# Memory-augmented attention and a spatial-gating MLP on one core: load phase reordered, half of a running sum moved ahead of the products with V

## The chip, the cores and the metric

The kernel runs on one core of a Trainium2 chip. The metric is the device time of one execution in microseconds (us), lower is better. Engines are named as in the profile: PE is TensorE (matmuls), PEld its weight loads, DVE is VectorE, ACT is ScalarE, POOL is GpSimd, SP is SyncE, which issues the DMAs. L514 is line 514 of the kernel.

## The reference

Block A is a recurrence over 64 segments of 32 tokens; 8 memory rows go ahead of each segment's tokens, and the first 8 rows of a segment's output are the memory of the next. Block B is an MLP with a gate that mixes over all 2048 tokens. Weights and activations are bfloat16; x is 2048 x 512, there are 32 heads of 128.

```python
for s in range(n_seg):
    xs = x[:, s * seg_len:(s + 1) * seg_len, :].copy()
    h = jnp.concatenate([mem, xs], axis=1)
    q = jnp.einsum('btd,dhe->bhte', h, Wq)
    k = jnp.einsum('btd,dhe->bhte', h, Wk)
    v = jnp.einsum('btd,dhe->bhte', h, Wv)
    scores = jnp.einsum('bhqe,bhke->bhqk', q, k) * scale
    scores = jnp.where(mask[None, None], scores, -1000000000.0)
    p = _softmax(scores, axis=-1)
    o = jnp.einsum('bhqk,bhke->bhqe', p, v)
    o = jnp.einsum('bhte,hed->btd', o, Wo)
    mem = o[:, :M, :].copy()
    outs.append(o[:, M:, :])
...
h = x + _A_ref(_layernorm(x, axis=-1), A_mem0, A_Wq, A_Wk, A_Wv, A_Wo, A_seg_len)
h2 = h + _B_ref(_layernorm(h, axis=-1), B_w_in, B_w_sp, B_b_sp, B_w_out)
```

## The kernel before

Every operation is written in one hand-made order. An `Emitter` records each operation with what it reads and writes, puts it at the end of its engine's list, and derives the semaphore waits. So an engine does its operations strictly in the order of the code, and the code's order is the schedule.

**Load phase.** `load_w` and `load_wh` bring Wq in quarters and Wk as two quarters and a half. Meanwhile PE computes, for the extension rows (the last 8 tokens of each segment, gathered for 16 segments in a "ck"), the Q and K products in 28 groups of 16 matmuls 128x128 (`qkx_mm`, L432): index n of the loop over `first` counts them. Groups 0 to 15 are Q, 16 to 27 are K. Each group writes one of four PSUM banks in turn, and its bank is emptied (`qkx_evac`) by ACT for even n (L441), by DVE for odd n (L443). So group n can begin only once group n-4 has been copied out. Between the groups DVE also normalizes three loaded blocks of x: `ln_stats` is a bn_stats (L379) and a bn_aggr (L380) on DVE followed by an add and a power on POOL (L381, L383); `ln_apply` (L389) on DVE needs POOL's result. A normalized block is turned by PE (`xT`, 16 matmuls, L397) and copied to the ring of x by ACT (`ring_copy`, `xe_copy`).

**Loop.** 64 iterations s, four to a row block rb = s // 4, with j4 = s % 4. In each, PE does the projections Q and K (L514 and L515 are one helper, `tile_mm`), the scores, two softmaxes (b = 0, 1), the projection V, and then this part, to which the change belongs:

- `ev`: one group of 16 matmuls from a list of work that is independent of the recurrence. It is `vx_group` for s = 1 to 7 and s = 10, 11, `qkx_group` for s = 8, 9, `qkr_group` for s = 12 to 43, and `z_group` (block B) from s = 44 until these run out, after s = 61.
- `PV_half(s, 0)` and `PV_half(s, 1)`: the products with V, for each half 16 matmuls 32x40 (L659) and 4 of 32x64 (L665). They need V (`V_evac`, L651 on DVE, L649 on ACT) and the normalized exponentials (L625, L631).
- `cT_evac`: four copies of 128x320 out of PSUM, 0 and 1 by ACT (L678), 2 and 3 by DVE (L680).
- `WoX_mm(rb - 1, j4)`, from s = 4 on: the first "ext output sum". The previous row block's extension rows are multiplied with Wo and summed in bank `WXB` over j4 = 0 to 3: eight matmuls of 512 columns (L743), four for each b. It reads `cTx`, which the four iterations of the row block before have filled.
- `late`: a group of four matmuls (`pour`). Where the `ev` group is a `vx_group`, it is done ahead of `ev`; else it stands here, behind `WoX_mm`.
- `Wo`: the output projection from `cT`, in the order 0, 2, 1, 3, in groups of four matmuls of 256 columns. The first group needs copy 0.

A matmul whose output has 32 rows stands in one of four column strips of the array; four of them, one per strip, run side by side and are called a group here.

**Places of the instruction stream.** `plan` (L1072) counts PE's instructions in blocks of `FETCH` = 256, and chooses for each iteration how many weight reloads (`spare`, four instructions each, 0 to 8 of them) to put in, so that a block's limit falls on certain places of the iteration. The instructions of an iteration that it assumes are written in it as a number.

## Time and profile before

| | |
|---|---|
| time, median of 3 runs | 840.41 us (838.03 to 840.58) |
| the profiled execution | 840.04 us, of which the span is 838.3 us |
| TensorE clock granted, mean | 0.999 |
| load phase, until the first matmul of the loop | 35.5 us |
| loop | 35.5 to about 683 us, about 9.9 us for an iteration |
| block B | from there to the end |

A row of the timeline has the start in us from the span's start, how long the merged row was busy, engine, line, operation, output and inputs, shape, count, and in brackets the idle time before it and what ended it. [...]

### The profile page before, as it was taken

To read this page: it belongs to the slowest core of one execution; us is meant where nothing else is said; L and a number is where in the kernel's file an instruction comes from. 1 tells how busy PE (TensorE), PEld (TensorE's weight loads), DVE (VectorE), ACT (ScalarE), POOL (GpSimd) and SP (SyncE) were. 2 spreads that over 40 slices of the span, in tenths; PEclk is the share of its full clock that TensorE was granted. 3 is DMA by queue.
4 is the path that set the end of the run, shared out by engine and by line. 5 is a ranking of instruction groups with operands and counts; after the bars stand their busy time and mean duration, and the time that the engine had idled before them with its cause. 6 is when DMAs were issued, how large, how long until landed. Compare 5 with 4: busy or idle time off the path is not lost.

```text
span 838.3 us, 45576 instructions
## 1 busy us (share of the span) xinstructions
PE 827.7 (99%) x22059; PEld 446.4 (53%) x19541; DVE 518.2 (62%) x1321; ACT 465.7 (56%) x1250; POOL 128.0 (15%) x340
## 2 busy tenths in 40 slices
PE   9999999999999999999999999999999999999997
PEld 9755555555555555555555555555555554444443
DVE  3556667666666666666666676666666667654443
ACT  3456665667666766667666666666666676500000
POOL 5011111111111111111111121111111113200000
PEclk9999999999999999999999999999999999999999
DMA  9962222323222212131223233233323389033001
GB/s 316 395 211 54 73 67 60 76 57 61 60 46 60 54 48 65 43 67 51 63 62 88 54 78 75 78 84 81 93 78 75 84 241 345 1 114 113 26 14 40
DMA packets 112407, 78.65 MB, mean 94 GB/s; under 512 B 65992, under 2 KB 103888, under 8 KB 112208
## 3 DMA queue, kind: packets, MB, share of 16 engines
q1 hardware_dynamic: 112208, 75.67, 31.7%
q8 instruction: 165, 2.70, 1.4%
q14 instruction: 34, 0.28, 0.1%
HBM read 43.16 MB, written 22.12 MB: 78 GB/s over the span
## 4 chain that ended last, share of the span: by engine, by line
PE 95%; DMA 1%; DVE 1%; ACT 1%; SPq 0%; issue 0%; POOL 0%
PE f_ps L514 47%; PE f_ps L1356 11%; PE f_ps L515 11%; PE f_ps L743 4%; PE f_ps L659 3%; PE f_ps L1480 3%; PE f_ps L1349 2%; PE f_ps L811 2%; PE f_ps L451 2%; PE f_ps L432 2%; DMA f_part<-in_A_x_dram 1%; PE f_ps L585 1%; PE f_ps L606 1%; PE f_ps L716 1%; PE f_ps L457 1%; PE f_ps L665 1%
## 5 line engine op out<-in xcount | busy, mean ns | idle before, releaser
L514 PE MATMUL f_ps<-f_arena,f_hT 128*32 128x512 bf16 (+1 forms) x5404 | 359.3, 351 | 0.3
L514 PEld LDWEIGHTS f_ps<-f_arena,f_hT 128*32 128x32 bf16 x5404 | 135.4, 96 | 138.7 <-issue 50.2
L551 ACT ACTIVATE f_Tst<-f_ps 128x512 bf16<-128x512 f32 x224 | 127.1, 597 | 65.3 <-PE f_ps L514 65.3
L515 PE MATMUL f_ps<-f_arena,f_hT 128*32 128x512 bf16 (+1 forms) x1764 | 146.7, 341 | 0.0
L514 PE MATMUL f_ps<-f_arena,f_cT 128*32 128x256 bf16 x3844 | 128.5, 272 | 0.9 <-ACT f_cT L678 0.5
L514 PEld LDWEIGHTS f_ps<-f_arena,f_cT 128*32 128x32 bf16 x3844 | 94.0, 96 | 28.9 <-ACT f_cT L678 19.6
L563 DVE STREAM_TRANSPOSE f_QT<-f_Tst 128x256 uint32<-128x256 uint32 x128 | 57.1, 446 | 72.2 <-ACT f_Tst L551 72.2
L1356 PE MATMUL f_ps<-f_arena 128*128 128x512 bf16 x448 | 101.0, 379 | 0.6 <-DVE f_arena L1342 0.4
L651 DVE CAST f_V_sb<-f_ps 128x512 bf16<-128x512 f32 (+1 forms) x128 | 71.0, 555 | 42.0 <-PE f_ps L514 42.0
L680 DVE TENSOR_SCALAR f_cT<-f_ps 128x320 bf16<-128x320 f32 x128 | 56.9, 487 | 28.6 <-PE f_ps L665 28.6
L1356 PEld LDWEIGHTS f_ps<-f_arena 128*128 128x128 bf16 x448 | 43.5, 98 | 54.0 <-DVE f_arena L1342 2.0
L599 ACT ACTIVATE f_E_sb<-f_ps 128x224 bf16<-128x224 f32 x128 | 46.2, 361 | 36.4 <-PE f_ps L591 36.4
L709 DVE CAST f_part<-f_ps 128x256 bf16<-128x256 f32 x64 | 27.2, 425 | 62.9 <-PE f_ps L514 62.9
L570 POOL COPY f_QT<-f_arena 128x128 uint32<-128x128 uint32 x64 | 18.8, 294 | 297.0 <-PE f_ps L591 296.9
L678 ACT ACTIVATE f_cT<-f_ps 128x320 bf16<-128x320 f32 x128 | 49.0, 435 | 23.0 <-PE f_ps L665 23.0
L721 ACT ACTIVATE f_hT<-f_ps 128x16 bf16<-128x16 f32 x126 | 23.2, 184 | 53.9 <-PE f_ps L716 53.4
L1362 DVE TENSOR_TENSOR f_arena<-f_ps,f_arena 128x512 f32<-128x512 f32 x28 | 19.3, 690 | 51.4 <-PE f_ps L1356 48.7
L575 DVE CAST f_ps<-f_mask 128x224 f32<-128x224 bf16 x128 | 47.1, 368 | 0.0
L621 ACT ACTIVATE f_R_sb<-f_R_sb 128x160 f32<-128x160 f32 x128 | 43.2, 338 | 4.1
L700 POOL COPY f_cTx<-f_cT 128x256 bf16<-128x256 bf16 x64 | 25.4, 398 | 121.7 <-DVE f_cT L680 121.7
L707 ACT ACTIVATE f_part<-f_ps 128x256 bf16<-128x256 f32 x64 | 24.6, 385 | 32.1 <-PE f_ps L514 32.1
L541 ACT ACTIVATE f_Tst<-f_ps 128x256 bf16<-128x256 f32 x128 | 42.1, 381 | 0.1
(130 smaller groups left out, 1206.9 us busy)
## 6 DMA issues: line engine op xcount, KB each, us to landing
wT_d<-f_wst SPq DMA_DIRECT2D x64, 128.0 KB, 2.7
f_arena<-wT_d SPq DMA_DIRECT2D x32, 256.0 KB, 4.9
f_arena<-in_A_Wv_dram SPq DMA_DIRECT2D x2, 2048.0 KB, 20.5
f_arena<-in_A_Wo_dram SPq DMA_DIRECT2D x8, 512.0 KB, 9.4
f_Vx<-vext_d SPq DMA_DIRECT2D x63, 64.0 KB, 2.4
f_arena<-in_A_Wq_dram SPq DMA_DIRECT2D x3, 1024.0 KB, 10.5
vext_d<-f_Vs SPq DMA_DIRECT2D x24, 128.0 KB, 2.2
z2p_d<-f_Vs SPq DMA_DIRECT2D x26, 112.0 KB, 1.9
```

The costliest lines, as they stand in the source:

```text
L514: return e.matmul(out, lhsT=lhsT, rhs=rhs, start=start, stop=stop, skip_group_check=True, tile_position=(0, 32 * c))
L515: return e.add_instruction(mybir.InstMatmult(name=nc.get_next_instruction_name(), ins=[e.lower_ap(rhs), e.lower_ap(lhsT)], outs=[e.lower_a ...
L541: act(lambda e: e.activation(out=Tst[:, 1, 256 * k:256 * k + 256].rearrange("p (gi r) -> p gi r", r=2), in_=ps[:, bank, 0:256].rearrange(" ...
L551: act(lambda e: e.activation(out=Tst[:, tb, :].rearrange("p (C gi r) -> p C gi r", C=2, r=2), in_=ps[:, bank, :].rearrange("p (C r gi) -> ...
L563: dve(lambda e: e.transpose(out=dst, in_=Tst[:, mi, :].bitcast(U32)), reads=[("T", mi, 0), ("T", mi, 1)], writes=wr)
L575: dve(lambda e: e.tensor_copy(out=ps[:, bank, 0:224], in_=mask[:, :]), reads=["mask"], writes=[PB(bank)])
L599: act(lambda e: e.activation(out=E_sb[:, b, :], in_=ps[:, bank, 0:224], func=ACT.Exp, scale=scale, bias=SHIFT), reads=[PB(bank)], writes=[ ...
L621: act(lambda e: e.activation(out=R_sb[:, b, :], in_=R_sb[:, b, :], func=ACT.Exp, scale=-1.0, bias=RBIAS), reads=[("R", b)], writes=[("R", b)])
L651: dve(lambda e: e.tensor_copy(out=V_sb[:, b, cs], in_=ps[:, bank, cs]), reads=[PB(bank)], writes=wr)
L678: act(lambda e: e.activation(out=dst, in_=src, func=ACT.Copy, scale=UNSC), reads=[PB(PVB[c])], writes=[("cT", c)])
L680: dve(lambda e: e.tensor_scalar(out=dst, in0=src, scalar1=UNSC, scalar2=None, op0=ALU.mult), reads=[PB(PVB[c])], writes=[("cT", c)])
L1356: pe(lambda e: e.matmul(ps[:, bank, 0:TB], lhsT=z2[:, sc, fb * 128:(fb + 1) * 128], rhs=wTb[tb % 2][:, :, sc, :], start=(n == 0), stop=(n ...
```

## The change

Load phase: the K groups of the two ck, which came as four of ck 0 and then four of ck 1, now alternate two by two. The three `ln_stats` move from behind groups 10, 11, 12 to behind 11, 12, 13, and the three `ln_apply` from behind 11, 12, 13 to behind 13, 14, 15, where they stand ahead of the `ln_stats` of the same n. The three turnings of x move from behind groups 15, 18, 21 to 17, 19, 22.

Loop: for s from 4 on, the left 256 columns of the first four of the eight matmuls of `WoX_mm` are done by four matmuls of their own (`WoX_first`) between `ev` and `PV_half(s, 0)`; the right 256 columns of the same four, and the other four at full width, stay behind the copies (`WoX_rest`). So there are 12 matmuls in the place of 8. The planner's count of an iteration rises from 592 to 600.

```diff
-    def WoX_mm(rb, qr):
-        for bg in range(8):
+    def WoX_first(rb, qr):
+        for g in range(4):
+            h = 4 * qr + g
+            pe(lambda e, h=h, g=g: e.matmul(ps[32 * g:32 * g + 32, WXB, 0:256], lhsT=cTx[:, rb % 2, 8 * qr + g, :], rhs=w_o[:, h, 0:256],
+                                            start=(qr == 0), stop=False, skip_group_check=True, tile_position=(0, 32 * g)),
+               reads=[("cTx", rb % 2), ("Wo", 0, qr)], writes=[PB(WXB)])
+
+    def WoX_rest(rb, qr):
+        for g in range(4):
+            h = 4 * qr + g
+            pe(lambda e, h=h, g=g: e.matmul(ps[32 * g:32 * g + 32, WXB, 256:512], lhsT=cTx[:, rb % 2, 8 * qr + g, :], rhs=w_o[:, h, 256:512],
+                                            start=False, stop=False, skip_group_check=True, tile_position=(0, 32 * g)),
+               reads=[("cTx", rb % 2), ("Wo", 0, qr)], writes=[PB(WXB)])
+        WoX_mm(rb, qr, range(4, 8))
+
+    def WoX_mm(rb, qr, bgs=range(8)):
+        for bg in bgs:
...
     first = [(ck, i) for i0 in range(0, 8, 2) for ck in range(2) for i in (i0, i0 + 1)]
-    first += [(0, i) for i in range(8, 12)] + [(1, i) for i in range(8, 12)] + [(0, i) for i in range(12, 16)]
+    first += [(ck, i) for i0 in (8, 10) for ck in range(2) for i in (i0, i0 + 1)] + [(0, i) for i in range(12, 16)]
...
+        if 13 <= n < 16:
+            ln_apply(n - 9)
         if 11 <= n < 14:
-            ln_apply(n - 7)
-        if 10 <= n < 13:
-            ln_stats(n - 6)
-        if n == 15:
+            ln_stats(n - 7)
+        if n == 17:
             xT(4, 6)
             ring_copy(0, 6)
-        if n == 18:
+        if n == 19:
             xT(5, 7)
             ring_copy(1, 7)
-        if n == 21:
+        if n == 22:
             xT(6, 6)
...
-        n = 592 + 24 * (s % 4 == 2) + 8 * (s >= 3 * CK)
+        n = 600 + 24 * (s % 4 == 2) + 8 * (s >= 3 * CK)
...
+        if rb > 0:
+            WoX_first(rb - 1, j4)
         PV_half(s, 0)
         PV_half(s, 1)
...
         if rb > 0:
-            WoX_mm(rb - 1, j4)
+            WoX_rest(rb - 1, j4)
```

DVE in the load phase, from its first copies of groups on. L443 are the copies of the odd groups. Before:

```order
L443 CAST f_arena<-f_ps 128x4x16x8 x5
L379 BN_STATS f_st<-f_part 128x6
L380 BN_AGGR f_mv<-f_st 128x2
L443 CAST f_arena<-f_ps 128x4x16x8
L389 TENSOR_SCALAR f_part<-f_part,f_mv,f_rs 128x512
L379 BN_STATS f_st<-f_part 128x6
L380 BN_AGGR f_mv<-f_st 128x2
L389 TENSOR_SCALAR f_part<-f_part,f_mv,f_rs 128x512
L379 BN_STATS f_st<-f_part 128x6
L380 BN_AGGR f_mv<-f_st 128x2
L443 CAST f_arena<-f_ps 128x4x16x8
L389 TENSOR_SCALAR f_part<-f_part,f_mv,f_rs 128x512
```

And now:

```order
L443 CAST f_arena<-f_ps 128x4x16x8 x6
L379 BN_STATS f_st<-f_part 128x6
L380 BN_AGGR f_mv<-f_st 128x2
L379 BN_STATS f_st<-f_part 128x6
L380 BN_AGGR f_mv<-f_st 128x2
L443 CAST f_arena<-f_ps 128x4x16x8
L389 TENSOR_SCALAR f_part<-f_part,f_mv,f_rs 128x512
L379 BN_STATS f_st<-f_part 128x6
L380 BN_AGGR f_mv<-f_st 128x2
L389 TENSOR_SCALAR f_part<-f_part,f_mv,f_rs 128x512
L443 CAST f_arena<-f_ps 128x4x16x8
L389 TENSOR_SCALAR f_part<-f_part,f_mv,f_rs 128x512
```

Between the copies of groups 11 and 13 stood two L389, each of which waits for POOL, and two pairs of statistics; now two pairs of statistics stand there and no L389.

PE in one iteration of the `qkr_group` kind, from the `ev` group (the L514 that reads f_hTe) to the first matmuls of `Wo` (the L514 that reads f_cT). Before:

```order
L514 MATMUL f_ps<-f_arena,f_hTe 32x512 x16
L659 MATMUL f_ps<-f_E_sb,f_V_sb 128x40 x16
L665 MATMUL f_ps<-f_E_sb,f_Vx 128x4x16 x4
L659 MATMUL f_ps<-f_E_sb,f_V_sb 128x40 x16
L665 MATMUL f_ps<-f_E_sb,f_Vx 128x4x16 x4
L743 MATMUL f_ps<-f_arena,f_cTx 32x512 x8
L451 MATMUL f_ps<-f_arena,f_hTe 32x512 x4
L514 MATMUL f_ps<-f_arena,f_cT 32x256 x32
```

And now (L742 is `WoX_first`, L749 the right half in `WoX_rest`, L758 `WoX_mm`):

```order
L514 MATMUL f_ps<-f_arena,f_hTe 32x512 x16
L742 MATMUL f_ps<-f_arena,f_cTx 32x256 x4
L659 MATMUL f_ps<-f_E_sb,f_V_sb 128x40 x16
L665 MATMUL f_ps<-f_E_sb,f_Vx 128x4x16 x4
L659 MATMUL f_ps<-f_E_sb,f_V_sb 128x40 x16
L665 MATMUL f_ps<-f_E_sb,f_Vx 128x4x16 x4
L749 MATMUL f_ps<-f_arena,f_cTx 32x256 x4
L758 MATMUL f_ps<-f_arena,f_cTx 32x512 x4
L451 MATMUL f_ps<-f_arena,f_hTe 32x512 x4
L514 MATMUL f_ps<-f_arena,f_cT 32x256 x32
```

Four matmuls of 256 columns now stand ahead of the products with V, and one group's half less stands between these and `Wo`.

More of the change, by code (lines that the diff above doesn't have):

```diff
@@ L743, in WoX_mm @@
             pe(lambda e, h=h, g=g, i=8 * qr + bg: e.matmul(ps[32 * g:32 * g + 32, WXB, :], lhsT=cTx[:, rb % 2, i, :], rhs=w_o[:, h, :],
-                                                           start=(i < 4), stop=(i >= H - 4), tile_position=(0, 32 * g)),
+                                                           start=(i < 4), stop=(i >= H - 4), skip_group_check=True, tile_position=(0, 32 * g)),
                reads=[("cTx", rb % 2), ("Wo", b, qr)], writes=[PB(WXB)])
```

## The prediction

> **What bounds the kernel now.** First the page: its span, the engines' shares, the chain that ended last.

> ```profile
> span 838.3 us, 45576 instructions
> PE 827.7 (99%) x22059; PEld 446.4 (53%) x19541; DVE 518.2 (62%) x1321; ACT 465.7 (56%) x1250; POOL 128.0 (15%) x340
> PE 95%; DMA 1%; DVE 1%; ACT 1%; SPq 0%; issue 0%; POOL 0%
> ```

> PE sets the end nearly everywhere, so an edit pays only where it removes time in which PE does not start the next matmul. The profiled execution took 840.04 us, 1.74 us of it outside the span; the median of three is 840.41, and single runs spread over 2.5 us. The sum below is made against 840.04.

> Second, PE's timeline of the load phase, between the eighth microsecond and the start of the loop.

> ```profile
> 8.37 13.62 PE L432 MATMUL f_ps<-f_hTe,f_arena 128*128 128x128 bf16 x240
> 21.92 0.41 PE L397 MATMUL f_ps<-f_ident,f_part 128*32 128x128 bf16 x16
> 22.26 1.07 PE L432 MATMUL f_ps<-f_hTe,f_arena 128*128 128x128 bf16 x16
> 24.49 1.96 PE L432 MATMUL f_ps<-f_hTe,f_arena 128*128 128x128 bf16 x32 [1.16 <-DVE f_arena L443]
> ```

> Fifteen groups take 21.92 - 8.37 = 13.55 us, 0.90 each. Group 16 starts at 22.26, so group 17 was due at 23.16; it starts at 24.49, 1.33 late, released by a DVE copy. DVE's timeline says why:

> ```profile
> 18.66 0.70 DVE L443 CAST f_arena<-f_ps 128x512 bf16<-128x512 f32 x1
> 20.36 0.41 DVE L389 TENSOR_SCALAR f_part<-f_part,f_mv,f_rs 128x512 bf16<-128x512 bf16 x1 [1.01 <-POOL f_rs L383]
> 20.69 0.69 DVE L379 BATCH_NORM_STATS2 f_st<-f_part 128x6 f32<-128x512 bf16 x1
> 22.59 0.41 DVE L389 TENSOR_SCALAR f_part<-f_part,f_mv,f_rs 128x512 bf16<-128x512 bf16 x1 [1.00 <-POOL f_rs L383]
> 23.74 0.69 DVE L443 CAST f_arena<-f_ps 128x512 bf16<-128x512 f32 x1
> ```

> The copy of group 13 runs from 23.74 to 24.43, behind two L389 that each waited 1 us for POOL. Group 17 needs its bank.

> Third, the same stretch of the loop, from the products with V (L659) to `Wo`, for each kind of iteration: s = 25 (`qkr_group`), with ACT's row of copies 0 and 1 last; then s = 45 (`z_group`), s = 5 (`vx_group`) and s = 8 (`qkx_group`).

> ```profile
> 300.35 1.04 PE L514 MATMUL f_ps<-f_arena,f_hTe 128*32 128x512 bf16 x16
> 301.32 0.27 PE L659 MATMUL f_ps<-f_E_sb,f_V_sb 32*128 32x40 bf16 x16
> 301.43 0.19 PE L665 MATMUL f_ps<-f_E_sb,f_Vx 32*128 32x64 bf16 x4
> 301.51 0.31 PE L659 MATMUL f_ps<-f_E_sb,f_V_sb 32*128 32x40 bf16 x16
> 301.79 0.61 PE L743 MATMUL f_ps<-f_arena,f_cTx 128*32 128x512 bf16 x8
> 302.23 0.39 PE L451 MATMUL f_ps<-f_arena,f_hTe 128*32 128x512 bf16 x4
> 302.45 1.04 PE L514 MATMUL f_ps<-f_arena,f_cT 128*32 128x256 bf16 x32
> 303.32 0.28 PE L515 MATMUL f_ps<-f_arena,f_cT 128*32 128x256 bf16 x4
> 301.89 0.77 ACT L678 ACTIVATE f_cT<-f_ps 128x320 bf16<-128x320 f32 x2 [0.35 <-PE f_ps L665]
> ```

> ```profile
> 501.00 0.27 PE L659 MATMUL f_ps<-f_E_sb,f_V_sb 32*128 32x40 bf16 x16
> 501.41 0.61 PE L743 MATMUL f_ps<-f_arena,f_cTx 128*32 128x512 bf16 x8
> 502.04 0.50 PE L514 MATMUL f_ps<-f_arena,f_cT 128*32 128x256 bf16 x12
> 501.53 0.77 ACT L678 ACTIVATE f_cT<-f_ps 128x320 bf16<-128x320 f32 x2 [0.38 <-PE f_ps L665]
> ```

> ```profile
> 102.28 0.27 PE L659 MATMUL f_ps<-f_E_sb,f_V_sb 32*128 32x40 bf16 x16
> 102.39 0.19 PE L665 MATMUL f_ps<-f_E_sb,f_Vx 32*128 32x64 bf16 x4
> 102.42 0.28 PE L659 MATMUL f_ps<-f_E_sb,f_V_sb 32*128 32x40 bf16 x16
> 102.68 0.62 PE L743 MATMUL f_ps<-f_arena,f_cTx 128*32 128x512 bf16 x8
> 103.29 0.40 PE L514 MATMUL f_ps<-f_arena,f_cT 128*32 128x256 bf16 x8
> 102.81 0.77 ACT L678 ACTIVATE f_cT<-f_ps 128x320 bf16<-128x320 f32 x2 [0.51 <-PE f_ps L665]
> ```

> ```profile
> 132.29 0.27 PE L659 MATMUL f_ps<-f_E_sb,f_V_sb 32*128 32x40 bf16 x16
> 133.35 0.28 PE L514 MATMUL f_ps<-f_arena,f_cT 128*32 128x256 bf16 x4
> L678 ACT ACTIVATE f_cT<-f_ps x128: 431/435/443, 51.7 to 681.5; 128x320 bf16<-128x320 f32 x128
> ```

> Two things are to be seen. In s = 25 the second half of the products starts 0.08 after the last L665 row, in s = 5 only 0.03 after: it is held, for V or the exponentials, and with the waits inside it the stretch from L659 to L743 is 0.47 long against 0.40. And in s = 5 the 8 matmuls of L743 cannot fill the time to `Wo`: two groups end their share at 103.12, and `Wo` starts at 103.29. Copy 0 ended at 102.81 + 0.435 = 103.245, 0.045 before. So **copy 0 is a floor: `Wo` starts no earlier than 103.29 - 102.28 = 1.01 after the products start**, when these run unheld. s = 25 takes 1.13, s = 45 1.04, s = 8 1.06.

> **The load phase.** No instruction is added. In the new order DVE has the copy of group 11 (at most until 18.66 + 0.70 = 19.36), two pairs of statistics (20.69 to 22.59 less the wait of 1.00 is 0.90 a pair, so until 21.2) and then the copy of group 13, until 21.9. Group 17 is now due at 21.83 + 0.90 = 22.73, since the turning of x (0.34) comes after it. The three L389 follow, with POOL's result long there; the copy of 15 is over by about 24.1 (L389, statistics, L389, copy: 0.33 + 0.90 + 0.33 + 0.69 after 21.9), group 19 due at 24.9. The turnings find their blocks ready. K's weights:

> ```profile
> 9.74 2.54 SPq L310 DMA_DIRECT2D f_arena<-in_A_Wk_dram  x2
> f_arena<-in_A_Wk_dram SPq DMA_DIRECT2D x2, 1024.0 KB, 12.6
> f_arena<-in_A_Wk_dram SPq DMA_DIRECT2D x1, 2048.0 KB, 16.6
> ```

> The two quarters land about 12.6 after issue, around 22 to 24; the half, issued at 12.3, near 28.9. The second quarter was wanted by group 18 and is now wanted by group 20, at about 26.3; the half by group 24, at 30.5. Neither binds. The term is **-1.33**, at worst 0 if the wait only moves on.

> **The loop: what the moved half costs.** Eight groups of 256 columns take 303.32 - 302.45 = 0.87, 0.109 each; a 512 group takes (302.23 - 301.79)/2 = 0.22. Two halves thus cost as much as one whole, and the added matmuls themselves nothing (0.002 by nanoseconds would be 0.1 us in all). [...]

> What matters is the order. The half ahead delays the products by its 0.109 (the change to the products' tiling is paid after it as it was after the group before: L514 of 300.35 starts its fourth group at 301.00, the products follow 0.32 later, 0.10 over the pitch). Behind the products 0.109 less stands before `Wo`, and the floor of 1.01 takes over. The time from the end of `ev` to `Wo` changes per kind of iteration:

> - `vx_group`, s = 4 to 7, 10, 11: already on the floor; +0.109 each, 6 times: **+0.65**.
> - `qkx_group`, s = 8, 9: the group ahead is 128 columns and full tiling, so a change of tiling is added, about 0.10; then 1.06 falls to 1.01: 0.109 + 0.10 - 0.05 = 0.16, twice: **+0.3**.
> - `qkr_group`, s = 12 to 43: the products start later, V and the exponentials are there, so the hold of 0.07 goes. Unhindered, PE would reach `Wo` 1.13 - 0.07 - 0.109 = 0.95 after their start; the floor makes it 1.01. Change: 0.109 + 1.01 - 1.13 = -0.01, 32 times: between -0.6 and 0 by the rounding of the rows, taken **-0.2**.
> - `z_group`, s = 44 to 58: 1.04 falls to 1.01, +0.08 to +0.09, 15 times: **+1.3**. s = 59 to 61, with 512 columns and 1.06: **+0.2**.
> - s = 62, 63: no `ev` of that kind; there the products wait for POOL, and the half is hidden in that wait:

> ```profile
> 680.51 0.27 PE L659 MATMUL f_ps<-f_E_sb,f_V_sb 32*128 32x40 bf16 x16 [0.67 <-POOL f_E_sb L625]
> ```

> Sum of the loop +2.3, between +1.6 and +2.9. Behind `Wo` everything moves along. `WoX_first` waits for nothing: its inputs were finished an iteration or more before. No DMA and no SP or POOL operation of the loop changes place.

> **Forecast**: -1.33 + 2.3 = +1.0, so 841.0 against 840.04 and 841.4 against 840.41; taken **841.2**, no change by the 0.3% (2.5 us) that a measurement of this kernel tells.

> **Rivals.**
> 1. *The copies are no floor* (faster). If copy 0 could end as soon as the products' earlier end lets PE come, `qkr_group` would gain another 0.06 to 0.08 (32 times, -2.2), `z_group` would be even instead of +0.09 (-1.3): -2.5 in all, 837.7. Against it: ACT starts copy 0 0.53 after the products' start in s = 5 and s = 45 alike, ACT idle before it. 7%.
> 2. *Instruction blocks* (slower). PE's stream comes by DMA:

> ```profile
> q8 instruction: 165, 2.70, 1.4%
> 461.02 0.21 PE L659 MATMUL f_ps<-f_E_sb,f_V_sb 32*128 32x40 bf16 x5 [0.21 <-issue]
> ```

> 165 transfers of 16 KB, about one per 256 of PE's 41,600 matmuls and weight loads. In the middle of a row of equal matmuls PE stands still here, waiting for nothing shown, at a block's limit: 0.21 idle, and about 0.16 more that the length of the matmul before it hides (0.19 in the L665 rows). 480 instructions are added and the reloads rise from 141 to 178, so every limit lands elsewhere. If a limit in or near the products (17 iterations now, 16 before, by counting) stalled each second time by 0.37, +3 comes on top: 844. Before, of the 16 only the one shown lost that much, so the stalls should stay near what they are; the point is reached only if the later blocks find the DMA engines busier. 10%. [...]
> 3. *The load wait only moves* to a later group, because POOL or the weights are late: 842.5, still no change. 8%.
> 4. *The added matmuls cost their own issue*: the 16 of L659 need 0.11, 0.007 each; 240 of them 1.7, on top of the forecast 842.9. 3%.

> Left for the forecast: 72%. Faster by over 0.3% (below 837.9) comes from rival 1 and a little luck with blocks: 0.08. Slower (above 842.9) from rival 2, half of 4 and the forecast's upper tail with more stalls: 0.16. Same: 0.76. The range 838.9 to 843.4 leaves out most of rivals 1 and 2.

> **What would show it.** In the load phase group 17 without a wait and the loop starting at about 34.2 instead of 35.5. In the loop, for s = 25 the second half of the products directly behind the first, and `Wo` 1.01 after the products; the iteration as long as before, within 0.01. For s = 45 an iteration 0.08 to 0.09 longer, PEld or PE waiting for ACT's L678. Wrong would be: `Wo` sooner than 1.0 after the products, a products' stretch still 0.47 long, or stalls by "issue" that together exceed those of before by over 1 us.

## The result, and the profile after

The changed kernel took 843.67 us (median of six runs, 841.97 to 845.99), the one before 839.5 beside it (six runs, 838.03 to 840.58): ratio 1.0051, 95% interval 1.0039 to 1.0062. It is slower by about half a per cent, where no change was forecast. The traced execution took 843.21, of which the span is 841.5, 3.2 more than before.

First the page of the changed kernel: its span, the shares, the share of PE in the chain that ended last, and the instruction queue.

```profile
span 841.5 us, 46186 instructions
PE 830.7 (99%) x22299; PEld 452.7 (54%) x19909; DVE 517.9 (62%) x1321; ACT 464.9 (55%) x1250; POOL 127.7 (15%) x340
...
q8 instruction: 167, 2.74, 1.4%
...
PE 98%; ACT 1%; DVE 0%; issue 0%; POOL 0%; POOLq 0%
```

PE is still what ends last. It has 240 matmuls more (22299 against 22059), and its stream comes in 167 transfers of q8 where it was 165.

Second, the load phase: PE's timeline from the first group, then DVE's around the place of the old wait.

```profile
7.62 1.06 PE L432 MATMUL f_ps<-f_hTe,f_arena 128*128 128x128 bf16 x16
...
8.94 15.50 PE L432 MATMUL f_ps<-f_hTe,f_arena 128*128 128x128 bf16 x272
...
34.82 0.40 PE L514 MATMUL f_ps<-f_arena,f_hT 128*32 128x512 bf16 x4
...
21.35 0.70 DVE L443 CAST f_arena<-f_ps 128x512 bf16<-128x512 f32 x1
21.94 0.40 DVE L389 TENSOR_SCALAR f_part<-f_part,f_mv,f_rs 128x512 bf16<-128x512 bf16 x1
```

The wait of group 17 is gone: from 8.94 on 17 groups (272 matmuls) run in one piece, and the three L389 wait for nothing. From the first group to the loop it is 34.82 - 7.62 = 27.20 now, 35.487 - 6.972 = 28.515 before: -1.31, as forecast. But the first group began 0.65 later than before (7.62 against 6.97), and that is not the change's doing. It hangs on the 40 matmuls of L891 (L906 now) that PE does first, called the warm-up here. Before, then now:

```profile
1.08 4.46 PE L891 MATMUL f_ps<-f_onesrc 128*128 128x160 bf16 x40 [1.08 <-POOL f_onesrc L335]
5.79 0.41 PE L397 MATMUL f_ps<-f_ident,f_xn 128*32 128x128 bf16 x16 [0.26 <-DVE f_xn L389]
```

```profile
1.07 5.43 PE L906 MATMUL f_ps<-f_onesrc 128*128 128x160 bf16 x40 [1.07 <-POOL f_onesrc L335]
6.44 0.41 PE L397 MATMUL f_ps<-f_ident,f_xn 128*32 128x128 bf16 x16
```

The same 40 matmuls of 160 columns last 4.46 in the one execution and 5.43 in the other; a second trace of the changed kernel, below, has 4.85, begins its first group at 7.03 and the loop at 34.22, where the prediction had 34.2.

What the load edits are worth depends on this start. With the old order, in eight traces, the first group begins anywhere from 6.89 to 7.76, and the loop from 35.34 to 35.57: a late first group only makes the wait of group 17 shorter (1.16 idle in `before`, 0.32 in `split_again`, below), because the copy it waits for stands behind POOL's L383, which ends at 20.3 in both. With the new order a late first group is passed on in full: from it to the loop it is 27.18 to 27.20 in ten of eleven traces. So the edits gain 1.3 where the first group is early and about 0.6 where it is late, as in the trace shown (34.82 against 35.49).

Third, the loop. L742 is `WoX_first`, L749 and L758 are `WoX_rest`. PE's rows overlap, so distances are taken from start to start: in s = 25 of the kernel before, a matmul of 512 columns lasts 0.379 and the next group begins 0.216 after its own, with 256 columns 0.272 and 0.109; the four matmuls of such a group begin within 0.011 of each other. Now s = 25 and s = 45, each with ACT's row of copies 0 and 1 last:

```profile
301.66 0.28 PE L742 MATMUL f_ps<-f_arena,f_cTx 128*32 128x256 bf16 x4
301.88 0.27 PE L659 MATMUL f_ps<-f_E_sb,f_V_sb 32*128 32x40 bf16 x16
301.99 0.20 PE L665 MATMUL f_ps<-f_E_sb,f_Vx 32*128 32x64 bf16 x4
302.02 0.28 PE L659 MATMUL f_ps<-f_E_sb,f_V_sb 32*128 32x40 bf16 x16
...
302.28 0.29 PE L749 MATMUL f_ps<-f_arena,f_cTx 128*32 128x256 bf16 x4
...
302.61 0.39 PE L451 MATMUL f_ps<-f_arena,f_hTe 128*32 128x512 bf16 x4
302.89 0.73 PE L514 MATMUL f_ps<-f_arena,f_cT 128*32 128x256 bf16 x20
...
302.40 0.77 ACT L678 ACTIVATE f_cT<-f_ps 128x320 bf16<-128x320 f32 x2 [0.41 <-PE f_ps L665]
```

```profile
502.29 0.27 PE L659 MATMUL f_ps<-f_E_sb,f_V_sb 32*128 32x40 bf16 x16
...
503.30 0.51 PE L514 MATMUL f_ps<-f_arena,f_cT 128*32 128x256 bf16 x12
...
502.81 0.77 ACT L678 ACTIVATE f_cT<-f_ps 128x320 bf16<-128x320 f32 x2 [0.49 <-PE f_ps L665]
```

In both, `Wo` starts 1.01 after the products (302.89 - 301.88, 503.30 - 502.29). In the trace's nanoseconds this distance is 1013 to 1015 from s = 1 to s = 61 in every iteration but three, in which something else holds PE longer; copy 0 ends 0.052 before `Wo`. The copy is the floor, as the prediction said, and the products run unheld (302.02 begins 0.03 behind the L665 row; before it was 0.08).

Where, then, is the rest? The loop took 608.53 before and 612.39 now, counted from the last group ahead of this part of s = 1 (ahead of the products, and of `WoX_first`) to the same place of s = 62. For each of six stretches of an iteration take the median over the iterations of its kind and its j4, and add these up: call that the **distances**, what every such iteration pays. What single iterations have above their median is the **pauses**. Before: 605.41 and 3.12. Now: 608.56 and 3.83. So the distances grew by 3.15, where 2.3 was forecast, and the pauses by 0.7. (A part of the pauses, some 0.5, stands in all traces alike, such as one wait in s = 7.)

By kind the distances grew by 0.64 in the six iterations with `vx_group`, 0.38 in the two with `qkx_group`, 0.46 in the 32 with `qkr_group`, 1.47 in the 15 with `z_group`, and 0.21 in s = 59 to 61.

The surprise is `qkr_group`. Up to `Wo` it is what the prediction had: the products start 0.109 later and `Wo` follows 0.114 sooner. But then two small things do not move along. Where `Wo` starts at the floor, its second group starts 0.120 after the first instead of 0.109, in every iteration. And every fourth, with j4 = 3, has another floor. ACT and the L716 row of `mem_out` in s = 23, before and now (L551 copies the `ev` group out, L748, now L763, the ext output sum, L707 the output that `mem_out` reads):

```profile
282.01 0.77 ACT L678 ACTIVATE f_cT<-f_ps 128x320 bf16<-128x320 f32 x2 [0.35 <-PE f_ps L665]
282.66 0.60 ACT L551 ACTIVATE f_Tst<-f_ps 128x512 bf16<-128x512 f32 x1
283.14 0.62 ACT L748 ACTIVATE f_partx<-f_ps 128x512 bf16<-128x512 f32 x1
283.66 0.38 ACT L707 ACTIVATE f_part<-f_ps 128x256 bf16<-128x256 f32 x1
...
282.56 1.05 PE L514 MATMUL f_ps<-f_arena,f_cT 128*32 128x256 bf16 x32
...
284.10 0.21 PE L716 MATMUL f_ps<-f_G_sb,f_part 128*32 128x8 bf16 x8
```

```profile
282.48 0.77 ACT L678 ACTIVATE f_cT<-f_ps 128x320 bf16<-128x320 f32 x2 [0.41 <-PE f_ps L665]
283.13 0.60 ACT L551 ACTIVATE f_Tst<-f_ps 128x512 bf16<-128x512 f32 x1
283.61 0.62 ACT L763 ACTIVATE f_partx<-f_ps 128x512 bf16<-128x512 f32 x1
284.09 0.42 ACT L707 ACTIVATE f_part<-f_ps 128x256 bf16<-128x256 f32 x1
...
282.97 1.06 PE L514 MATMUL f_ps<-f_arena,f_cT 128*32 128x256 bf16 x32
...
284.56 0.21 PE L716 MATMUL f_ps<-f_G_sb,f_part 128*32 128x8 bf16 x8
```

ACT runs without a gap from copy 0 to L707, so `mem_out` comes 2.08 to 2.09 after copy 0 starts, both times. Before, that was when PE arrived anyway (1.54 after `Wo`); now `Wo` is nearer to copy 0, PE arrives sooner, and waits (1.59). That is 0.04 more in each of eight iterations.

The pauses show in the view of waits (what PE waited for, total, times, longest), of before and of now, as waits for issue:

```profile
PE f_ps L514 <- issue: 0.3, 1, 0.3
PE f_ps L659 <- issue: 0.2, 1, 0.2
```

```profile
PE f_ps L716 <- issue: 0.6, 2, 0.3
PE f_ps L514 <- issue: 0.6, 2, 0.3
```

One of them in the timeline, s = 28:

```profile
334.24 0.20 PE L716 MATMUL f_ps<-f_G_sb,f_part 128*32 128x8 bf16 x5
334.78 0.18 PE L716 MATMUL f_ps<-f_G_sb,f_part 128*32 128x8 bf16 x3 [0.34 <-issue]
```

The eight matmuls of `mem_out` are cut after the fifth. Counted through PE's stream, the cut lies where the prediction's block limits lie, one instruction in 256; the step is 0.50 longer than the same step in other iterations, of which the row's 0.34 is what the matmul before, 0.166 long, does not hide.

### The profile page after: what moved, and what is told of

Same layout as the page of the kernel before. It is cut to its first block, busy times and chain, and to the rows that moved or that the text cites. A ratio compares the mean times of both kernels' runs of the same rounds, so it can differ in the third digit from the quotient of the medians.

```text
span 841.5 us, 46186 instructions
## 1 busy us (share of the span) xinstructions
PE 830.7 (99%) x22299; PEld 452.7 (54%) x19909; DVE 517.9 (62%) x1321; ACT 464.9 (55%) x1250; POOL 127.7 (15%) x340
## 4 chain that ended last, share of the span: by engine, by line
PE 98%; ACT 1%; DVE 0%; issue 0%; POOL 0%; POOLq 0%
PE f_ps L514 48%; PE f_ps L1373 11%; PE f_ps L515 10%; PE f_ps L432 4%; PE f_ps L1497 3%; PE f_ps L659 3%; PE f_ps L826 2%; PE f_ps L1366 2%; PE f_ps L451 2%; PE f_ps L758 1%; PE f_ps L585 1%; PE f_ps L749 1%; PE f_ps L606 1%; PE f_ps L716 1%; PE f_ps L457 1%; PE f_ps L742 1%
## 5 line engine op out<-in xcount | busy, mean ns | idle before, releaser
L514 PE MATMUL f_ps<-f_arena,f_hT 128*32 128x512 bf16 (+1 forms) x5532 | 360.8, 351 | 0.6 <-issue 0.3
L514 PEld LDWEIGHTS f_ps<-f_arena,f_hT 128*32 128x32 bf16 x5532 | 138.8, 96 | 135.6 <-issue 46.0
L551 ACT ACTIVATE f_Tst<-f_ps 128x512 bf16<-128x512 f32 x224 | 127.1, 597 | 65.9 <-PE f_ps L514 65.9
L515 PE MATMUL f_ps<-f_arena,f_hT 128*32 128x512 bf16 (+1 forms) x1636 | 136.5, 342 | 0.0
L514 PE MATMUL f_ps<-f_arena,f_cT 128*32 128x256 bf16 x3844 | 128.8, 273 | 2.2 <-ACT f_cT L678 1.0
L514 PEld LDWEIGHTS f_ps<-f_arena,f_cT 128*32 128x32 bf16 x3844 | 91.6, 96 | 35.3 <-ACT f_cT L678 26.1
L709 DVE CAST f_part<-f_ps 128x256 bf16<-128x256 f32 x64 | 27.2, 425 | 61.7 <-PE f_ps L514 61.7
L678 ACT ACTIVATE f_cT<-f_ps 128x320 bf16<-128x320 f32 x128 | 49.0, 435 | 27.4 <-PE f_ps L665 27.1
L707 ACT ACTIVATE f_part<-f_ps 128x256 bf16<-128x256 f32 x64 | 24.9, 389 | 31.4 <-PE f_ps L514 31.4
## 6 DMA issues: line engine op xcount, KB each, us to landing
wT_d<-f_wst SPq DMA_DIRECT2D x64, 128.0 KB, 2.7
f_arena<-in_A_Wv_dram SPq DMA_DIRECT2D x2, 2048.0 KB, 20.5
f_arena<-in_A_Wq_dram SPq DMA_DIRECT2D x3, 1024.0 KB, 11.3
vext_d<-f_Vs SPq DMA_DIRECT2D x24, 128.0 KB, 2.3
```

What stands on the lines that cost most here:

```text
L514: return e.matmul(out, lhsT=lhsT, rhs=rhs, start=start, stop=stop, skip_group_check=True, tile_position=(0, 32 * c))
L515: return e.add_instruction(mybir.InstMatmult(name=nc.get_next_instruction_name(), ins=[e.lower_ap(rhs), e.lower_ap(lhsT)], outs=[e.lower_a ...
L551: act(lambda e: e.activation(out=Tst[:, tb, :].rearrange("p (C gi r) -> p C gi r", C=2, r=2), in_=ps[:, bank, :].rearrange("p (C r gi) -> ...
L678: act(lambda e: e.activation(out=dst, in_=src, func=ACT.Copy, scale=UNSC), reads=[PB(PVB[c])], writes=[("cT", c)])
```

## The experiments

Two theories stood against each other. **Order**: the moved half is paid ahead of the products, and floors set by ACT's copies keep PE from getting it back. **Blocks**: the added instructions, and the new places of the blocks' limits, make PE pause. A ratio stands to the kernel before of the same batch of runs, whose median lay between 839.3 and 840.1.

### One part at a time

`load_only` has the load edits alone, `loop_only` the loop edits with the planner's 600.

> Only the edits of the load phase. Load theory (the wait of group 17 on DVE's copy of group 13 is 1.33 and is really gained): 1.3 under the kernel before, to within the 0.6 by which the warm-up of the start may differ; groups to loop 28.5 before, 27.2 here. 'The wait only moves': 0. If this kernel is 1.3 faster, the loop edits must cost about 5.5 of the change's +4.2; if it is 0, they cost 4.2.

> Only the edits of the loop, with the planner's 600. Order theory (copy 0 is the floor, the half ahead is paid as far as the floor takes over, with the costs per kind that the changed kernel's trace shows): +3.1 against before. Block theory (new places of the blocks' limits stall PE more): another +1 to +2.5 on top, and then seen as pauses in the trace at limits, over 1 us more in all than before. The prediction had +2.3.

`load_only`: 839.08 against 840.02, ratio 0.9989 (0.998 to 0.9997). `loop_only`: 844.98, ratio 1.006 (1.0045 to 1.0075). The parts add up, -0.9 and +5.0 to the change's +4.2. So the load edits gain, by somewhat less than the 1.33, and the loop edits cost twice the 2.3. In the trace of `loop_only` the distances are 3.36 longer than before, the pauses 1.96. Its distances are the changed kernel's; both theories have a share.

### How much goes ahead, and where

All three keep the load edits, and have something ahead only in s = 12 to 43.

```diff
+        ahead = 12 <= s < 44
+        if ahead:
+            WoX_first(rb - 1, j4)
...
-            WoX_mm(rb - 1, j4)
+            (WoX_rest if ahead else WoX_mm)(rb - 1, j4)
```

`WoX_first` has 256 columns, 128, or 512. With 512 no matmul is split and none added.

> The edits of the load phase, and 256 columns ahead of the products only in the 32 iterations with qkr_group (s = 12 to 43). Order theory: -1.3 for the load, +0.2 for qkr_group, +0.3 for the waits of mem_out at every fourth iteration: -0.8 against before. Block theory: as the full change minus the costs of places, so that the loss goes with the number of added instructions (256 of 480): +1.5.

> As the kernel with 256 columns in s = 12 to 43, with 128 columns ahead and 384 behind, the same number of instructions. Order theory: the hold of the products goes as with 256, but PE comes to Wo 0.055 later, so the floor is only just reached: some 0.04 to 0.05 less per iteration than with 256, 32 times: -2.6 to -3.0 against before. Block theory, or a price of added instructions: the same time as with 256 columns, within 0.5.

> The edits of the load phase, and the first four matmuls whole (512 columns) ahead of the products in s = 12 to 43, so that no matmul is added and the planner counts as before. Order theory with copy 0 as the floor: each of the 32 iterations pays another 0.109 against 256 columns and gets nothing back, +3.5 against that kernel: about +3.6 against before. If the copies were no floor, or if the added matmuls or their blocks were what costs: no more than with 256 columns, +0.1 or less.

256 columns: 840.48 against 840.02, ratio 1.0001 (0.999 to 1.0012). 128: 839.17, ratio 0.9987 (0.9977 to 0.9997). 512: 841.63 against 839.27, ratio 1.0026 (1.0016 to 1.0037). s = 25 with 128 columns, then with 512:

```profile
300.15 0.23 PE L742 MATMUL f_ps<-f_arena,f_cTx 128*32 128x128 bf16 x4
300.31 0.27 PE L659 MATMUL f_ps<-f_E_sb,f_V_sb 32*128 32x40 bf16 x16
...
300.45 0.31 PE L659 MATMUL f_ps<-f_E_sb,f_V_sb 32*128 32x40 bf16 x16
...
301.33 1.05 PE L514 MATMUL f_ps<-f_arena,f_cT 128*32 128x256 bf16 x32
```

```profile
302.38 0.39 PE L742 MATMUL f_ps<-f_arena,f_cTx 128*32 128x512 bf16 x4
302.71 0.27 PE L659 MATMUL f_ps<-f_E_sb,f_V_sb 32*128 32x40 bf16 x16
...
303.33 0.39 PE L451 MATMUL f_ps<-f_arena,f_hTe 128*32 128x512 bf16 x4
303.72 1.06 PE L514 MATMUL f_ps<-f_arena,f_cT 128*32 128x256 bf16 x32
```

With 512 columns `Wo` is again 1.01 behind the products, although the last group behind them, L451, was begun 0.39 ahead of it: 0.17 over a group's pitch of 0.22, spent on nothing but copy 0. The distances of the 32 iterations grow by 3.86 over before, by 3.3 over 256 columns: the floor, shown from its other side. In the time only 2.4 is left of the distances' 4.2, since the load edits gain up to 1.3 and this kernel has the fewest pauses of all (1.9 in the trace). With 128 columns the products still wait a little inside (the second half of 300.45 lasts 0.31), PE reaches `Wo` 1.02 behind them, and the 32 iterations are 1.14 shorter than before: here the idle time of the hold is really used, without being lost at the floor. The order theory has every sign right. But 256 columns came out at +0.5 where it had -0.8, and 128 at -0.9 where it had -2.6 to -3.0: the pauses of both traces, 4.8 and 4.2, are over a microsecond longer than before.

`late_behind` takes 128 columns ahead also in s = 4 to 7, 10 and 11, and moves `late` there behind the sum (`full = s > 3 and bool(gx)`).

> As the kernel with 128 columns ahead in s = 12 to 43, and the same also in s = 4 to 7, 10 and 11, where the group late now stands behind the first ext output sum instead of ahead of ev. Order theory: in these six PE waited about 0.1 for copy 0, and the group now fills this time: between -0.05 and -0.1 each, so -0.3 to -0.6 against the kernel with 128 columns, about -1.3 against before. If there is nothing to fill: the same as with 128 columns.

838.65 against 839.27, ratio 0.9996 (0.9987 to 1.0005): a miss in the time. The distances fell by 2.1 against before, 1.0 more than with 128 columns, and nearly all of it comes from the six iterations, 0.16 each, which is more than was expected. A pause in s = 62, behind the stretch counted here, gives 0.2 back, and the pauses within it are 0.8 longer than before. No version beats the kernel before by more than 128 columns do, and that one is not to be told from `load_only`.

### The traces once more

> The changed kernel once more, unaltered. Order theory: the same distances in every iteration (Wo 1.01 after the products, mem_out 0.04 late at every fourth iteration), 3.7 to 4.2 over before. For the pauses at limits of instruction blocks: if the place of a limit decides, the pauses of the first trace (0.48 in s = 28, 0.50 in s = 46, 0.46 in s = 50) come back at the same limits; if it is chance, others do, with a sum of 1 to 3.

> The kernel before once more, for a second trace. If the place of a limit decides on the pauses, 0.52 in s = 43 and 0.37 in s = 41 come back; if chance, others do. The distances of the loop outside these pauses: the same within 0.1 in sum.

The changed kernel: 842.82 against 839.27, ratio 1.004 (1.0027 to 1.0053). The distances repeat within 0.05 (608.61 and 608.56; before 605.38 and 605.41). The pauses repeat in part: of the three named, s = 28 came back with 0.25 instead of 0.50, s = 46 with the same 0.50, s = 50 not at all; those of s = 35 and s = 42 came back, and new ones are in s = 16, 24 and 36. In the kernel before neither the 0.37 nor the 0.52 came back. So place plays a part and chance another. All of them lie at block limits.

### The instructions without the order

`split_only` is the kernel before with the four matmuls split into halves, both behind the products, and the planner's 600: the added instructions and their places, without the order.

```diff
         if rb > 0:
-            WoX_mm(rb - 1, j4)
+            WoX_first(rb - 1, j4)
+            WoX_rest(rb - 1, j4)
```

> The kernel before with the first four matmuls of the first ext output sum split into halves of 256 columns, all of them behind the products as before, and the planner's 600: the change's 480 added instructions and its places of the blocks' limits without its order, and without the load edits. Order theory alone: the distances stay as before, 0 within 0.3. Block theory: the pauses at limits add up to 3.0 to 4.3 as in the kernels with the loop edits, instead of 2.1 to 2.2: +0.8 to +2. A price of the matmuls' own issue: +1.7, seen as longer distances in every iteration.

> The kernel with the four matmuls split and all behind the products once more, for a second trace. Block theory: distances outside the pauses as in the kernel before within 0.3, and pauses at limits of 3.5 to 5.5 that make up the difference in time. If the added matmuls have a price that the first trace hid: longer distances, by 0.05 an iteration or more.

843.58 against 840.09, ratio 1.0044 (1.0028 to 1.0061), and the second time 842.14 against 839.95, ratio 1.0035 (1.0023 to 1.0047). This was the run that mattered. s = 25:

```profile
302.40 0.27 PE L659 MATMUL f_ps<-f_E_sb,f_V_sb 32*128 32x40 bf16 x16
...
302.59 0.31 PE L659 MATMUL f_ps<-f_E_sb,f_V_sb 32*128 32x40 bf16 x16
...
302.87 0.29 PE L742 MATMUL f_ps<-f_arena,f_cTx 128*32 128x256 bf16 x4
...
303.53 1.05 PE L514 MATMUL f_ps<-f_arena,f_cT 128*32 128x256 bf16 x32
```

0.47 for the products and 1.13 to `Wo`, exactly as before. Over the loop the distances differ from the kernel before by 0.28 in the first trace and 0.13 in the second: the 240 added matmuls show no price of their own. The pauses are 5.45 and 4.39 instead of 3.12 and 2.89. In s = 28 the place of the changed kernel's pause has one again, in the first and in the second trace:

```profile
334.81 0.21 PE L716 MATMUL f_ps<-f_G_sb,f_part 128*32 128x8 bf16 x5
335.64 0.19 PE L716 MATMUL f_ps<-f_G_sb,f_part 128*32 128x8 bf16 x3 [0.62 <-issue]
```

```profile
334.88 0.20 PE L716 MATMUL f_ps<-f_G_sb,f_part 128*32 128x8 bf16 x5
335.43 0.18 PE L716 MATMUL f_ps<-f_G_sb,f_part 128*32 128x8 bf16 x3 [0.35 <-issue]
```

So a change that moves nothing, and lengthens no distance, costs 2.2 to 3.5 in the medians; the pauses of its two traces are 2.4 and 1.4 over the mean of the two of before.

### Trying to place the limits better

In the first ten traces pauses of more than 0.06 came only with blocks of 256 instructions that were used up in 4.0 us or less (92 of 722 such blocks, none of 737 longer ones, s = 1 to 61), and nearly all with a limit between the first ext output sum and the end of the second `mem_out`, called the dense part here: PE begins 63 matmuls and weight loads a us there and 60 in the rest of an iteration (medians of the kernel before). Two rules were made from this. The first puts weights on these places in the planner (`before_places`, `after_places`, `late_places`).

```diff
-        return 4 if 338 <= place < 378 else 1 if 318 <= place < 338 or 148 <= place < 196 else 0
+        if place < 44:
+            return 6 if place >= 4 else 11
+        r = place - extra - pv
+        return 11 if r >= 200 else 7 if 124 <= r < 162 else 9 if 74 <= r < 112 else 1 if 46 <= r < 74 else 0
```

Here `pv` is the place of the first product.

> The kernel before with other weights for the planner: heavy where the traces so far show pauses at limits (from the first groups of Wo over mem_out to the second mem_out of the next iteration), light at the products. Block theory: the pauses add up to 1.0 to 1.5 instead of 2.1 to 2.2, 0.5 to 1.2 faster than before. If the place of a limit does not matter: the same.

> The changed kernel with the same new weights. Block theory: the pauses add up to at most 1.5 instead of 3.0 to 3.3, so 1.5 to 2 faster than the changed kernel, and against the kernel before with the new weights only the order is left: -1.3 for the load and +3.2 for the loop, +1.8 to +2.0. If the place does not matter: as the changed kernel.

> The kernel with 128 columns ahead up to s = 43 and late behind the sum in s = 4 to 7, 10, 11, with the new weights. Block theory: pauses of at most 1.5 instead of 2.9, 1 to 1.5 faster than without the new weights, about -2 against before. If the place does not matter: -0.6 against before as without them.

840.92 against 840.09, ratio 1.0011 (1.0002 to 1.002); 843.07, ratio 1.0038 (1.0023 to 1.0053); 839.54, ratio 0.9997 (0.9986 to 1.0008). None got faster. The second rule replaces the planner by a list of reloads, worked out from the traces' distances so that few of the blocks that end in the dense part last under 3.7 us (2 instead of 19 before, 6 instead of 30 in the changed kernel).

```diff
-        spare[0] = plan(s, pe_count[0] + WAITS + STEP * s)[1] if s else 0
+        spare[0] = RELOADS[s]
```

> The kernel before with a fixed list of reloads in the place of the planner, chosen so that 2 instead of 19 blocks that end in the dense part of an iteration (from the first ext output sum to the second mem_out) last under 3.7 us. Block theory (a pause only where a block is used up faster than the next one comes): pauses of 0.5 to 1.2 instead of 2.1 to 2.2, 1 to 1.5 faster than before. If pauses come by chance or by place: the same as before.

> The kernel with the four matmuls split, all behind the products, with such a list (6 short blocks instead of 32). Block theory: the pauses fall from 4.2 to about 1.2, the kernel stands within 0.6 of the one before with its list, and 2.5 to 3.5 under the split kernel with the planner. A price of the added matmuls or instructions themselves: still +2 or more over the one before with its list.

> The changed kernel with such a list (6 short blocks instead of 30). Block theory: pauses of about 1.3 instead of 3.0 to 3.3, 1.5 to 2.5 faster than the changed kernel; against the kernel before with its list the order and the load are left, -1.3 + 3.2 = +1.9, within 0.6. If the pauses are not the cause: no faster than the changed kernel.

> The kernel with the load edits, 128 columns ahead up to s = 43 and late behind the sum, with such a list (9 short blocks instead of 33). Block theory: 1 to 2 faster than with the planner, 2 to 3 under the kernel before.

840.44 against 839.94, ratio 1.0003 (0.9995 to 1.0012); 842.04, ratio 1.0026 (1.0015 to 1.0038); 843.45, ratio 1.0042 (1.0029 to 1.0055); 840.73, ratio 1.0005 (0.9995 to 1.0015). The rule fails: the pauses in the traces are 3.8, 4.3, 2.7 and 6.6, and now come mostly with blocks of 3.7 to 4.0 us, a few with longer ones. The list of the kernel before adds 340 instructions (85 reloads of four) outside the dense part and costs 0.5 at most; the split, with 480 in the dense part (240 matmuls and their loads) and 128 of reloads, cost 2.2 to 3.5.

The traces hold what the rule left out: when each transfer of PE's instructions (q8, 16 KB, one block by the prediction's count) begins and when it has landed. At the limit in s = 28 at which six kernels pause, the block before was used up equally fast; what differs is how long ago the last transfer had landed:

| s = 28 | block used up in | limit reached, after the landing | pause | PE goes on, after the landing |
|---|---|---|---|---|
| changed kernel | 3.67 | 0.84 | 0.50 | 1.35 |
| the same again | 3.67 | 1.13 | 0.25 | 1.38 |
| loop_only | 3.67 | 0.69 | 0.73 | 1.42 |
| split_only | 3.67 | 0.65 | 0.78 | 1.44 |
| split_again | 3.67 | 0.78 | 0.51 | 1.30 |
| late_behind | 3.62 | 0.62 | 0.81 | 1.44 |

So it is in all 19 traces (s = 1 to 61). Of the limits that PE reached less than 1.0 after the landing, 67 of 68 brought a pause of more than 0.06; between 1.0 and 1.4, 136 of 249; later, 5 of 2467. After a pause PE goes on 1.16 to 1.63 after the landing, 1.40 in the median, and none of the 2784 limits was passed sooner than 1.16 after it. So a pause is read here as the wait for the next block, though no run moved a transfer by itself. The transfer begins 0.9 after the limit before in the median, but in s = 28 above 1.5 to 2.1 after it, and takes 0.9 to 1.4 in most cases: 2.0 + 1.0 + 1.4 is 4.4, and a block used up in 3.7 is then too short. That is how a list made by the length of the blocks alone could fail.

All traces together, in us, distances and pauses from s = 1 to s = 62:

| kernel | distances, against before | pauses |
|---|---|---|
| before, two traces | 0 and -0.03 | 3.1, 2.9 |
| load_only | 0.0 | 3.2 |
| before_places, before_list | -0.3, +0.1 | 3.0, 3.8 |
| ahead512_qkr | +4.2 | 1.9 |
| split_only, split_again | +0.3, +0.1 | 5.5, 4.4 |
| changed kernel, two traces | +3.15, +3.2 | 3.8, 4.3 |
| loop_only | +3.35 | 5.1 |
| ahead256_qkr, ahead128_qkr | +0.55, -1.1 | 4.8, 4.2 |
| late_behind | -2.1 | 3.8 |
| after_places, after_list | +3.3, +3.45 | 3.2, 2.7 |
| late_places, split_list, late_list | -1.95, +0.7, -1.3 | 4.2, 4.3, 6.6 |

Kernels with the planner's weights as they were and without added matmuls (four traces) have pauses of 2.8 in the mean, those with added matmuls (eight) 4.5.

## Why the prediction was wrong

- **The load phase: the mechanism right, the size only where the first group is early.** From the first group to the loop -1.31 against -1.33, but -0.9 in the medians of `load_only`, and -0.7 and -1.1 at the start of the loop in the changed kernel's two traces: the old order hides a late first group, the new one does not. In the trace of `load_only` another 0.44 is lost to a late quarter of Wq, in none of the other ten with these edits.
- **Copy 0 as a floor: right.** `Wo` is 1.01 behind the products in every kind of iteration, also with twice as much ahead. Rival 1 falls with it. `vx_group` (+0.64 against +0.65) and s = 59 to 61 (+0.21 against +0.2) are as forecast, `qkx_group` (+0.38 against +0.3) nearly.
- **"Behind `Wo` everything moves along": wrong.** `Wo`'s second group comes 0.01 later wherever the floor holds, and with j4 = 3 ACT's chain of copies is a second floor, for `mem_out`. `qkr_group` costs +0.46 to +0.49 instead of -0.2, `z_group` +1.48 instead of +1.3. The distances of the loop are +3.2 instead of +2.3. The mechanism was there; ACT's queue behind copy 0 should have been followed to its end: the rows of before show L707 over at 284.04 and `mem_out` at 284.10, no room at all.
- **"The stalls should stay near what they are": wrong, and by the medians of the split alone the larger error.** Rival 2 was given 10% and a price of 3; split alone it costs 2.2 to 3.5, and in the changed kernel's two traces the pauses are 0.8 to 1.3 above the mean of the two of before. The prediction counted only limits in or near the products. The first ten traces have 5 of their 92 pauses of more than 0.06 in the products; the others lie from the sum over `Wo` to the second `mem_out`, which it did not count. (Its count of reloads was off too: 128 weight loads came on top of the 240, that is 32 reloads more and not 37.) With half of the sum ahead, the pauses and the order stand side by side: this is a sum of two terms, not one in place of the other.
- **Rival 3** did not happen, no later group waited. **Rival 4** falls by `split_only`: distances unchanged.
- **The base** was 0.3 to 1.1 high: the medians of before were 839.3 to 840.1 over six batches, not 840.41.

In sum for the two traces of the changed kernel against the two of before: -0.7 and -1.1 for the load, +3.2 for the order, +0.7 and +1.4 for pauses, which is +3.2 and +3.5. The traced spans give 841.5 - 838.3 = 3.2 and 841.4 - 837.6 = 3.8; the medians give +4.2 and +3.6. So the medians are 1.0 and 0.1 over the sum. That the executions without a trace had longer pauses is likely, since the pauses differ by a microsecond from trace to trace, but it was not shown.

The traces show that pauses lie at block limits, that they add up to more with the split (5.5 and 4.4 against 3.1 and 2.9), and that they end about 1.4 after the last transfer of the stream has landed. That the length of the block alone decides is not so: the list made from it did not shorten them. What stays open is why one transfer begins 0.9 after the limit before and another 2; that busier DMA engines bring a stall, as the prediction supposed, no run shows.

## What to carry to other kernels

To move work ahead of a stage that another engine empties, follow that engine's queue to its last reader, not only to the first: here copy 0 was one floor and L707, at the end of ACT's chain, the next, with 0.06 of room before it. Ask how much idle time there is to fill (0.07 here), and move no more than that: in the distances 128 columns gained 1.1 where 256 lost 0.55, though in the time the kernel with 128 is not to be told from the load edits alone. And in a loop that keeps PE busy throughout, count instructions as a cost even where their matmuls lengthen no distance (480 with 128 of reloads cost 2.2 to 3.5 here): split a matmul only where it buys more than the pauses it may bring, and try the split without the move first. Where such pauses come, look in the trace at when the instruction transfers land before making a rule for the places.
